# Gated attention and a Hyena convolution in one kernel: the last output stores move to GpSimd's queue, the spectrum's transfers are shared between two queues, the last tile is split, and the planner gets other weights

## The chip, the cores and the metric

The kernel runs on one core of a Trainium2 chip. The time is the device time of one launch in microseconds (us), lower is better. The engines are called as in the profile: PE (TensorE, matmuls; PEld is its weight load), DVE (VectorE), ACT (ScalarE), POOL (GpSimd) and SP (SyncE, which only issues transfers). Each engine executes its own list of instructions in order; an instruction that waits holds up all that stand behind it on the same engine. A transfer is issued by one of the engines and counts as one of that engine's instructions.

## The reference

Batch B = 8, sequence S = 3136, width D = 256, width of the queries 64. The inputs are u, v, z, and the weights `w_proj`, `filter_fft`, `w_out`.

```python
def _attn_ref(u, v, z):
    scale = 1.0 / S
    scores = scale * np.matmul(z, z.transpose(0, 2, 1))
    attn = np.maximum(scores, 0.0) ** 2
    out = np.matmul(attn, v)
    return u * out

def _moe_ref(x, w_proj, filter_fft, w_out):
    proj = x @ w_proj
    x1, x2, x3 = proj[..., :D], proj[..., D:2*D], proj[..., 2*D:]
    X2 = np.fft.rfft(x2, n=S, axis=1)
    H = np.fft.rfft(filter_fft, n=S, axis=0)[None, :, :]
    x2_conv = np.fft.irfft(X2 * H, n=S, axis=1)
    y = x1 * x2_conv * x3
    return y @ w_out
```

The first function's result is the x of the second. The output has the shape (8, 3136, 256) in float32.

## The kernel before

**The work of a batch.** The 3136 columns of the score matrix are cut into seven chunks (512 five times, 256, 320). For each chunk, tiles of 128 rows of scores are computed by matmuls that use 64 rows of the array (z has 64 columns), two or four of them side by side in the halves or quarters of the array, into one of three pairs of PSUM banks (`ps_s`). ACT takes the relu into `R_t` (L1767), DVE (L1776) or ACT (L1774) squares it into `A_t`, and PE weighs v with it: matmuls of the full array into `ps_o_t`. All matmuls go through one helper and carry its line, L521. Some tiles are not computed but transposed from their mirror image (`M_t`, `M1_t`, `M2o_t`, `M2e_t`). When a chunk is through, DVE multiplies by u (`xT_t`, L1818), and three projections follow: two of them become a gate (a copy `x_t` by ACT, L554, and a product `gate_t` by DVE, L1160), and the third goes into the spectrum.

**The convolution.** It is a DFT of 3136 = 64 x 49 points as matrix products. The first step of each chunk yields `s_t`, which SP writes to a buffer D1 in DRAM (L964; the profile calls it `spec`). With all chunks of a batch written, `add_spectrum` loads it back in another order (`load_spec`, L994), does eight forward quads (matmuls of half the array), copies (L554 on ACT, L558 on DVE) into `xh`, multiplies with the filter's spectrum H on DVE (L1248), does the inverse quads, and writes the result to a second DRAM buffer, D2 (`put`, L1293; three transfers for each set of quads, cut by rows in `by_row`). `add_end` loads that (`load_c`, L1006), does the last DFT step (called conv below), multiplies with the gates on DVE (`yT_t`, L1334), multiplies with w_out, copies the result out of PSUM in tiles of two (L554, L558) and stores it (`store`, L1394: two transfers a chunk, one for each half of the rows).

**What sets the order.** The order of every engine's instructions is made when the program is built, by a planner in Python (classes `Task` and `Plan`). A task has a cost in microseconds for each engine that may do it (two engines for copies and squares), tasks that it depends on, buffers that it takes, `moves` (the time that its transfer occupies the modelled transfer engines) and `late` (an addition to the modelled arrival). `Plan.go` always starts the task that can begin first in the model, and so writes the lists. These estimates only decide the order and which of two engines does a copy or a square; on the chip semaphores guard the data. `pick_pe` chooses PE's next task among scores (S), quads (Q), weigh matmuls (W) and the convolution's and the output's matmuls (FA, FB, FZ), by the numbers of a `Rule`:

- `backlog`: how much weigh work must be waiting before other work is taken while scores wait for a PSUM pair
- `ample`: from how much waiting weigh work on scores are done in groups of three and not two
- `stay`: how long PE may wait for further scores before it leaves the half-array mode
- `first`: how much weigh work must be waiting for a quad to be put ahead of scores
- `lead`: how many scores must have run before a quad may follow in the same stretch
- `pace`: how much credit for other work each weigh task earns
- `full`: from which load of ACT and DVE on other work stands behind the weigh work
- `give`: in `pick`, the penalty on a second engine's taking over a task, for the time that it holds up tasks which only it can do

**The end of the program.** The last chunks of the last batch but one (from chunk `HOLD` = 3 on) are held back in the queue FZ, where they fill PE's gaps in the last batch; their outputs come from cut pieces of `v_t` (the class `Cut`) and from `ost_t`. The last batch (`final`) puts its spectrum in five sets, two quads, two, two, one and one, from the buffers `gs_t`, `gs_t`, `M2o_t`, `A_t` and `uT_t`. Its chunks end in the order `FINAL` = 0, 2, 4, 6, 1, 3, 5; there, with `split`, POOL stores the first half of the rows and SP the second, except for the last chunk, which SP stores in one piece for each pair of tiles. In the steady part SP issues all output stores, spectrum transfers and transposing loads, and POOL the loads of u (`un_t`, L595) and v (`v_t`, L614).

Of the kernel before, what the change touches and what calls it, by code (L numbers as in the profile page):

```python
# [27 lines left out]
LATE_PUT, LATE_LOAD, LATE_TURN, LATE_C, LATE_D2 = 3.0, 1.0, 1.5, 2.5, 1.0  # L28
SPEC_LAG = 1
LATE_F = 6.0  # L30
LATE_OUT = 2.0
AFTER = (1, 3, 5, 6)
FINAL = (0, 2, 4, 6, 1, 3, 5)
ZP, ZL = 0, 0.0
# [1 line left out]
REACH = 2  # L36
Rule = namedtuple("Rule", "backlog ample stay first lead pace full give")
STEP = 50.0
RULES = [Rule(0.5, 5.0, 0.15, 0, 1, 0.55, 3.5, 0)]
SHARE = {0: 1, 2: 3}  # L40

ISSUED = "issued"
# [349 lines left out]
def kernel(  # L392
# [10 lines left out]
    nc = tc.nc  # L403

    B, S, D = u.shape
# [9 lines left out]
    home = {t: c for c in range(NC) for t in tiles[c]}  # L415
# [8 lines left out]
    D2 = [dram.tile([NT * P, D], BF16, name=f"spec2_{i}") for i in range(2)]  # L424
# [123 lines left out]
    def on(engine, emit, cost, deps=(), takes=(), **kw):  # L548
        return job(None, lambda e: emit(), {engine: cost}, deps, takes, **kw)
# [168 lines left out]
    for i, (t0, t1) in enumerate(zip(z_cuts, z_cuts[1:])):  # L718
        step_ = -(-(t1 - t0) // -(-(t1 - t0) // 8))
        for g0 in range(t0, t1, step_):  # L720
            nt = min(step_, t1 - g0)
            box = {}
# [260 lines left out]
    def by_row(d, t, x0, n):  # L983
        rows = d[0:S, :].rearrange("(q r x) d -> r q x d", r=2, x=2 * NJ)[:, :, ds(x0, n), :]
        got = [(rows[r, 0:EVEN], t[ds(r * N1, EVEN), 0:n, :]) for r in range(2)]
        return got + [(rows[:, EVEN], t[EVEN : EVEN + N1 + 1 : N1, 0:n, :])]

    def load_spec(src, j0, nj, deps, late=0.0, home=l_p):
        box = {}

        def go():
            box["t"] = home.tile([P, 8, D], BF16)
            for rows, part in by_row(src, box["t"], 2 * j0, 2 * nj):
                nc.sync.dma_start(out=part, in_=rows)  # L994

        t = on("SP", go, 1.3, [*deps, *((d, ISSUED) for d in loads[-1:])], [home.slots], moves=0.6 * nj, late=late)
        return in_order(t), box

    def load_c(src, c, deps, home):
        t0, nt = T0[c], len(tiles[c])  # L1000
        box = {}

        def go():
            box["t"] = home.tile([P, 4, D], BF16)
            view = src[ds(t0 * P, nt * P), :].rearrange("(t p) d -> p t d", t=nt)
            nc.sync.dma_start(out=box["t"][:, 0:nt, :], in_=view)  # L1006

        if home is c_p:
            return in_order(on("SP", go, 0.45, [*deps, *((d, ISSUED) for d in loads[-1:])], [home.slots], moves=0.4 * nt, late=LATE_C)), box
        return on("SP", go, 0.45, deps, [home.slots], moves=0.4 * nt), box  # L1010

    def sides(x):
        return x[:, 0:D], x[:, D : 2 * D]
# [200 lines left out]
    def add_spectrum(b, puts):  # L1214
        deps0 = list(h_done) + list(tz_done) if b == 0 else []
        final = b == B - 1
        sets = [(0, 1), (2, 3), (4, 5), (6,), (7,)] if final else [(0, 1), (2, 3), (4, 5), (6, 7)]
        set_of = {g: x for x in sets for g in x}
        outs = [gs_p, gs_p, M_p[2], A_p, uT_p] if final else [gs_p] * 4
        homes = [l_p, l_p, *M_p[:2]]  # L1220
        lasts = []
        behind = []
        ldb, gb = [None], [None]
        for g in range(NJ // 2):
            own = not final or g % 2 == 0
            xh = xh_p if own else R_p
            mine = set_of[g]
            per, gh = 2 * len(mine), outs[sets.index(mine)]
            if g % 2 == 0:
                ldb[0] = load_spec(D1[b % 2], 2 * g, 4, puts, LATE_LOAD * (not final), homes[g // 2] if final else l_p)  # L1230
            ld, ibox = ldb[0]
            xb = {}

            def mm(ps, g=g, xb=xb, ibox=ibox, xh=xh):
                xb["x"] = xh.tile([P, 2, 4, D], BF16)
                forward(ps, slot(ibox["t"], 2 * g % 4), g)

            def ev(e, h, p, xb=xb):
                copy(e, xb["x"][:, 0, ds(2 * h, 2), :].rearrange("p c d -> p (c d)"), p)

            a0, evs = add_quads(mm, ev, c_quads(g), [ld, *deps0], [xh.slots])
            if g % 2:
                a0.frees.append((ld, 0))

            def mul(i, g=g, xb=xb):
                x = xb["x"][:].rearrange("p i (j c) d -> p i j c d", c=2)
                h = H[:, ds(2 * g, 2), i].unsqueeze(2).to_broadcast([P, 2, 2, D])
                nc.vector.tensor_tensor(x[:, 1 - i], x[:, 0], h, ALU.mult)  # L1248

            def add(xb=xb):  # L1250
                x = xb["x"][:].rearrange("p i (j c) d -> p i c j d", c=2)
                nc.vector.tensor_tensor(x[:, 1, 0], x[:, 1, 0], x[:, 0, 1], ALU.subtract)
                nc.vector.tensor_tensor(x[:, 1, 1], x[:, 1, 1], x[:, 0, 0], ALU.add)

            cost = c_dve2(4 * D)
            w_ = on("DVE", lambda mul=mul: mul(0), cost, evs, prio=ZP)
            w_ = on("DVE", lambda mul=mul: mul(1), cost, [w_], prio=ZP, lat=ZL)
            z_ = w_ if final else on("DVE", add, 2 * c_dve2(2 * D), [w_], prio=ZP)

            def inv(g=g, xb=xb, z_=z_, a0=a0, gh=gh, mine=mine, per=per):  # L1260
                new = g == mine[0]
                if new:
                    gb[0] = {"es": [], "firsts": []}
                gx = gb[0]

                def mm(ps, g=g, new=new):
                    if new:
                        gx["g"] = gh.tile([P, 2 * per, D], BF16)
                    z, y = (slot(xb["x"][:, i], 0) for i in range(2))
                    if final:  # L1270
                        inverse2(ps, y, z, g)
                    else:
                        inverse(ps, y, g)

                def ev(e, h, p, g=g):
                    copy(e, gx["g"][:, ds(2 * (2 * (g - mine[0]) + h), 2), :].rearrange("p c d -> p (c d)"), p)

                a, evs = add_quads(
                    mm, ev, c_quads(g, 1 + final), [z_, *gx["firsts"], *(minus_task if final else [])], [gh.slots] if new else []
                )  # L1280
                gx["firsts"] = [a]
                if new:
                    gx["g0"] = a
                a.frees.append((a0, 1))
                inverses.append(a)
                gx["es"] += evs
                if g != mine[-1]:
                    return
                j0 = 2 * mine[0]

                def put():
                    for rows, part in by_row(D2[b % 2], gx["g"], 2 * j0, 2 * per):
                        nc.sync.dma_start(out=rows, in_=part)  # L1293

                p_ = on("SP", put, 1.2, gx["es"], moves=0.5 * per, late=LATE_D2 * (not final))
                p_.frees.append((gx["g0"], 1))
                lasts.append(p_)

            behind.append(inv)
            if g >= SPEC_LAG:  # L1300
                behind.pop(0)()
        for x in behind:
            x()
        return lasts

    def add_end(b, lasts, gtasks, cs, kind="FB", src=c_p, dsts=(o_p,), late=0, behind=(), then=(), split=False, mids=(y_p,)):
        for at, c in enumerate(cs):
            t0, nt = T0[c], len(tiles[c])
            w = CHUNKS[c]
            dst, mid = dsts[at % len(dsts)], mids[at % len(mids)]  # L1310
            ld, cb = load_c(D2[b % 2], c, lasts, src)
            yb = {}
            ys = []
            firsts = []
# [33 lines left out]
                ys.append(e_)  # L1348
            ob = {}
            oe = []  # L1350
            for i0 in range(0, nt, 2):
                n = min(2, nt - i0)
                last = min(P, w - (i0 + n - 1) * P)
                box = {}

# [34 lines left out]
            def store(i0, n, only=(0, 1), by=nc.sync, c=c, ob=ob):  # L1390
                r = rows_n1(out[b])
                for j, lo, hi, n2 in runs(T0[c] + i0, T0[c] + i0 + n):
                    if j in only:
                        by.dma_start(out=r[:, n2 : n2 + hi - lo, :], in_=ob["o"][ds(j * N1, N1), i0 : i0 + hi - lo, :])  # L1394

            if split and c == cs[-1]:
                for k, e_ in enumerate(oe):
                    s_ = on("SP", lambda i0=2 * k, n=min(2, nt - 2 * k), store=store: store(i0, n), 0.9, [e_, *behind], prio=1, moves=0.9)
            elif split:
                s_ = on("POOL", lambda nt=nt, store=store: store(0, nt, (0,), nc.gpsimd), 0.6, [*oe, *behind], moves=0.22 * nt)  # L1400
                s_ = on("SP", lambda nt=nt, store=store: store(0, nt, (1,)), 0.8, [*oe, *behind], prio=1, moves=0.22 * nt)
            else:
                s_ = on("SP", lambda nt=nt, store=store: store(0, nt), 1.3, [*oe, *behind], prio=1, moves=0.45 * nt, late=LATE_OUT * (dst is o_p))
# [508 lines left out]
```

## Time and profile before

| what | value |
|---|---|
| median of 3 runs | 992.51 us (992.26 to 992.87) |
| the profiled execution's own time | 993.72 us |
| its span | 991.5 us |
| mean granted clock of PE | 0.99 |
| packets under 512 B | 242442 of 332343 |
| mean transfer rate | 172 GB/s |
| relus on ACT, L1767 | 512, busy 466.9 us, mean 963 ns |
| squares on DVE, L1776 | 283 of the main form's group, 313.9 us, mean 1123 ns |
| squares on ACT, L1774 | 213 of the main form's group, 211.7 us, mean 1007 ns |
| copies `x_t` on ACT, L554 | 148, 81.7 us, mean 583 ns |
| multiplications with H on DVE, L1248 | 120, 82.0 us, mean 683 ns |

The page of the profile shows one execution, so its span is set against that execution's own time and not against the median. "Busy" is the time in which an engine executes; the sum over engines exceeds the span as they run side by side. The chain that ended last is put down to PE for 82% of the span, to DVE for 7% and to ACT for 4%. A row such as the relu's also names what the engine had waited for: ACT sat idle 57.1 us before relus, 55.0 of them for PE's scores.

### The profile page before, as it was taken

The page shows a single profiled execution, that of the slowest core. Times are in us where ns is not written, and L with a number is a line of the kernel's source. Part 1 is how long each engine was busy: PE and PEld are TensorE (multiplying, and loading weights), DVE is VectorE, ACT ScalarE, POOL GpSimd, SP SyncE. Part 2 cuts the span into 40 slices and gives each one's busy share as a digit, 9 for nine tenths or more (in the row PEclk, how much of TensorE's full clock was granted, in tenths as well). Part 3 has the DMA queues.
Part 4 walks back from the last instruction along what each step waited for, and adds up shares of the span by engine and source line. Part 5 has one row for each costly group of instructions (what it writes and reads, how often), then busy time and mean ns, then how long its engine had stood idle before and what let it go on. Part 6 is the DMA issues. An engine that isn't in the chain of part 4 may idle for free.

```text
span 991.5 us, 19534 instructions
## 1 busy us (share of the span) xinstructions
PE 958.2 (97%) x6831; PEld 472.2 (48%) x6831; DVE 819.4 (83%) x1465; ACT 867.9 (88%) x1187; POOL 191.7 (19%) x409
## 2 busy tenths in 40 slices
PE   6999999999999999999999999999999999999985
PEld 2344544455444554446444454444544455544643
DVE  7876689987899878987789877898779988799774
ACT  6988898988998898899989999889989899999773
POOL 5132311132013210313111220121202231001001
PEclk9999999999999999999999999999999999999978
DMA  9889958979979799978998786998889978984576
GB/s 154 150 171 199 165 118 128 187 137 185 202 174 176 147 194 187 186 156 133 200 197 178 148 152 152 205 191 158 153 196 186 203 138 165 202 213 106 154 229 197
DMA packets 332343, 170.32 MB, mean 172 GB/s; under 512 B 242442, under 2 KB 307786, under 8 KB 332244
## 3 DMA queue, kind: packets, MB, share of 16 engines
q1 hardware_dynamic: 304068, 136.59, 63.4%
q0 software_dynamic: 28176, 32.48, 23.2%
q8 instruction: 54, 0.88, 0.4%
q14 instruction: 45, 0.37, 0.1%
HBM read 90.26 MB, written 53.35 MB: 145 GB/s over the span
## 4 chain that ended last, share of the span: by engine, by line
PE 82%; DVE 7%; ACT 4%; DMA 2%; issue 2%; SPq 1%; POOL 0%; POOLq 0%; DVEq 0%; ACTq 0%
PE ps_o_t L521 48%; PE ps_s L521 34%; DVE A_t L1776 2%; ACT R_t L1767 2%; DVE xT_t L1818 1%; DMA M2e_t<-A_t 1%; DVE xh L1248 1%; DMA ost_t<-in_z_dram 1%; DMA conv_in_t<-spec 1%; DVE gate_t L1160 1%; DVE yT_t L1334 1%; SPq L646 1%; ACT A_t L1774 0%; ACT x_t L554 0%; DMA M_t<-A_t 0%
## 5 line engine op out<-in xcount | busy, mean ns | idle before, releaser
L1767 ACT ACTIVATE R_t<-ps_s 128x1024 f32<-128x1024 f32 (+4 forms) x512 | 466.9, 963 | 57.1 <-PE ps_s L521 55.0
L521 PE MATMUL ps_o_t<-A_t,v_t 128*128 128x512 bf16 (+3 forms) x2084 | 459.5, 354 | 2.9 <-DVE A_t L1776 2.1
L521 PEld LDWEIGHTS <-v_t 128*128 128x128 bf16 (+2 forms) x2878 | 250.6, 98 | 257.8 <-issue 73.2
L1776 DVE TENSOR_TENSOR A_t<-R_t 128x1024 bf16<-128x1024 f32 (+3 forms) x283 | 313.9, 1123 | 64.2 <-ACT R_t L1767 61.1
L1774 ACT ACTIVATE A_t<-R_t 128x1024 bf16<-128x1024 f32 (+3 forms) x213 | 211.7, 1007 | 3.1 <-DMA M2e_t<-A_t 1.7
L521 PE MATMUL ps_s<-zT_t 64*64 64x512 bf16 (+5 forms) x1485 | 170.8, 361 | 2.0 <-ACT R_t L1767 1.0
L604 POOL COPY tick<-xT_t 1x1 bf16<-1x1 bf16 x54 | 13.8, 256 | 681.6 <-DVE xT_t L1818 681.6
L521 PEld LDWEIGHTS <-zT_t 64*64 64x64 bf16 (+1 forms) x1518 | 53.9, 101 | 109.7 <-issue 93.7
L521 PE MATMUL ps_s<-xT_t,wp 128*128 128x512 bf16 (+2 forms) x430 | 103.7, 353 | 2.4 <-DVE gate_t L1160 0.9
L554 ACT ACTIVATE x_t<-ps_s 128x512 bf16<-128x512 f32 (+2 forms) x148 | 81.7, 583 | 19.7 <-PE ps_s L521 12.5
L1818 DVE SCALAR_TENSOR_TENSOR xT_t<-ps_o_t,uT_t 128x256 bf16<-128x256 f32 (+2 forms) x224 | 76.1, 381 | 22.8 <-PE ps_o_t L521 14.4
L1248 DVE TENSOR_TENSOR xh<-xh,H 128x1024 bf16<-128x1024 bf16 x120 | 82.0, 683 | 2.1 <-ACT xh L554 0.9
L521 PE MATMUL ps_o_t<-M_t,v_t 128*128 128x512 bf16 (+2 forms) x352 | 81.8, 353 | 0.0
L1160 DVE TENSOR_TENSOR gate_t<-ps_s,x_t 128x256 bf16<-128x256 f32 (+2 forms) x216 | 71.2, 381 | 6.6 <-PE ps_s L521 4.6
L1334 DVE TENSOR_TENSOR yT_t<-ps_s,gate_t 128x512 bf16<-128x512 f32 (+2 forms) x99 | 57.9, 613 | 10.3 <-PE ps_s L521 10.0
L558 DVE CAST xh<-ps_s 128x512 bf16<-128x512 f32 x71 | 47.3, 685 | 22.8 <-PE ps_s L521 19.5
L521 PEld LDWEIGHTS <-wp 128*128 128x128 bf16 x448 | 42.3, 98 | 49.6 <-issue 15.2
L595 POOL DMA_DIRECT2D un_t<-in_u_dram x112 | 59.8, 554 | 5.6 <-issue 2.7
L614 POOL DMA_DIRECT2D v_t<-in_v_dram x112 | 59.4, 552 | 6.4 <-issue 3.8
L521 PE MATMUL ps_s<-wp,xT_t 128*128 128x256 bf16 x398 | 56.7, 272 | 0.5 <-ACT R_t L1767 0.3
L521 PE MATMUL ps_s<-wo,yT_t 128*128 128x256 bf16 (+1 forms) x344 | 52.0, 273 | 1.6 <-DVE yT_t L1334 1.3
L554 ACT ACTIVATE s_t<-ps_s 128x512 bf16<-128x512 f32 (+1 forms) x79 | 44.9, 592 | 5.5 <-PE ps_s L521 2.1
(154 smaller groups left out, 833.1 us busy)
## 6 DMA issues: line engine op xcount, KB each, us to landing
out_dram<-ost_t SPq DMA_DIRECT2D x66, 256.0 KB
spec<-s_t SPq DMA_DIRECT2D x96, 128.0 KB
spec_in_t<-spec SPq DMA_DIRECT2D x60, 192.0 KB
spec<-gs_t SPq DMA_DIRECT2D x60, 192.0 KB
v_t<-in_v_dram POOLq DMA_DIRECT2D x80, 128.0 KB, 4.5
un_t<-in_u_dram POOLq DMA_DIRECT2D x80, 128.0 KB, 4.9
conv_in_t<-spec SPq DMA_DIRECT2D x33, 256.0 KB
out_dram<-ost_t SPq DMA_DIRECT2D x19, 128.0 KB
```

The lines of the kernel that those rows point to most:

```text
L521: wrote(nc.tensor.matmul(o, *args, **kw), o)
L554: got = nc.scalar.activation(out_, in_, AF.Copy)
L558: got = nc.vector.tensor_copy(out_, in_)
L595: nc.gpsimd.dma_start(out=t[ds(j * N1, N1), lo - t0 : hi - t0, :], in_=x[:, n2 : n2 + hi - lo, :])
L614: nc.gpsimd.dma_start(out=t[ds(j * N1, N1), ds(v_at(a), (b - a) * D)], in_=r[:, n2 + a - lo : n2 + b - lo, :].rearrange("p t d -> p (t d)"),)
L1160: got = nc.vector.tensor_tensor(g[:, ::-1] if h == 0 else g, p, x, ALU.mult)
L1248: nc.vector.tensor_tensor(x[:, 1 - i], x[:, 0], h, ALU.mult)
L1334: got = nc.vector.tensor_tensor(yb["y"][:, dh, 0:w], p, gates[b, c, dh][:, 0:w], ALU.mult)
L1767: has_read(nc.scalar.activation(blocks(box["R"], n, cw)[:rows], p, AF.Relu), p)
L1774: nc.scalar.activation(a, r, AF.Square)
L1776: nc.vector.tensor_tensor(a, r, r, ALU.mult)
L1818: nc.vector.scalar_tensor_tensor(x, f, inv_s2, ut, ALU.mult, ALU.mult)
```

## The change

Five things are edited; the rest of the code is the same.

1. The `Rule` has other numbers (`backlog` 0.5 to 1.25, `stay` 0.15 to 0.05, `first` 0 to 0.5, `pace` 0.55 to 0.5, `full` 3.5 to 3.0, `give` 0 to 1.0).
2. The planner's estimates of two loads are others: `load_spec` (issue 1.3 to 1.6, transfer 0.6 to 0.4 for each) and `load_c` outside its own pool (0.45 to 0.55, 0.4 to 0.3).
3. In the last batch each set's put to D2 is divided: SP issues the first one or two of its three transfers, POOL the rest. Over the five sets that makes eight by SP and seven by POOL.
4. All output stores of the last batch but one are issued by POOL, 14 of them after the last of POOL's loads.
5. The last chunk of the last batch (chunk 5, two tiles) computes, copies out and waits for its output tile by tile (`step` = 1); one half of its rows is stored by SP, the other by ACT.

```diff
+LATE_POOL = 1.2
...
-RULES = [Rule(0.5, 5.0, 0.15, 0, 1, 0.55, 3.5, 0)]
+RULES = [Rule(1.25, 5.0, 0.05, 0.5, 1, 0.5, 3.0, 1.0)]
...
-        t = on("SP", go, 1.3, [*deps, *((d, ISSUED) for d in loads[-1:])], [home.slots], moves=0.6 * nj, late=late)
+        t = on("SP", go, 1.6, [*deps, *((d, ISSUED) for d in loads[-1:])], [home.slots], moves=0.4 * nj, late=late)
...
-        return on("SP", go, 0.45, deps, [home.slots], moves=0.4 * nt), box
+        return on("SP", go, 0.55, deps, [home.slots], moves=0.3 * nt), box
...
-                def put():
-                    for rows, part in by_row(D2[b % 2], gx["g"], 2 * j0, 2 * per):
-                        nc.sync.dma_start(out=rows, in_=part)
-
-                p_ = on("SP", put, 1.2, gx["es"], moves=0.5 * per, late=LATE_D2 * (not final))
+                def put(part=slice(0, 3), by=nc.sync):
+                    for rows, t in by_row(D2[b % 2], gx["g"], 2 * j0, 2 * per)[part]:
+                        by.dma_start(out=rows, in_=t)
+
+                if final:
+                    n = 1 + mine[0] // 2 % 2
+                    p_ = on("SP", lambda: put(slice(0, n)), 0.55 * n, gx["es"], moves=0.25 * per)
+                    lasts.append(
+                        on("POOL", lambda: put(slice(n, 3), nc.gpsimd), 0.55 * (3 - n), gx["es"], moves=0.25 * per, late=LATE_POOL)
+                    )
+                else:
+                    p_ = on("SP", put, 1.2, gx["es"], moves=0.5 * per, late=LATE_D2)
...
+            step = 1 if split and c == cs[-1] else 2
...
-            for i0 in range(0, nt, 2):
-                n = min(2, nt - i0)
+            for i0 in range(0, nt, step):
+                n = min(step, nt - i0)
...
             if split and c == cs[-1]:
-                for k, e_ in enumerate(oe):
-                    s_ = on("SP", lambda i0=2 * k, n=min(2, nt - 2 * k), store=store: store(i0, n), 0.9, [e_, *behind], prio=1, moves=0.9)
+
+                def both_queues(nt=nt, store=store):
+                    store(0, nt, (0,))
+                    store(0, nt, (1,), nc.scalar)
+
+                s_ = on("SP", both_queues, 0.6, [*oe, *behind], prio=1, moves=0.45 * nt)
+            elif b == B - 2:
+                s_ = on(
+                    "POOL", lambda nt=nt, store=store: store(0, nt, by=nc.gpsimd), 1.2, [*oe, *behind],
+                    moves=0.45 * nt, late=LATE_POOL,
+                )
```

The planner's cost of a task and its `moves` enter the order of all engines, so the edits change the order outside the places that they name, too.

## Prediction

> **What bounds the kernel now.** I read the page's totals and its 40 slices first.
>
> ```profile
> span 991.5 us, 19534 instructions
> ...
> PE 958.2 (97%) x6831; PEld 472.2 (48%) x6831; DVE 819.4 (83%) x1465; ACT 867.9 (88%) x1187; POOL 191.7 (19%) x409
> ...
> PE   6999999999999999999999999999999999999985
> ...
> PEclk9999999999999999999999999999999999999978
> ```
>
> PE is busy throughout except in the first slice and the last two, and only there is the clock lower. So the span is PE's time plus a start (11.6 us idle in the first 50, which the change leaves alone: PE's order there is the same) plus a tail. I then cut the rest into stages, one row each: from:to, length, then PE, PEld, DVE, ACT and POOL busy (instructions), granted clock, DMA share, GB/s.
>
> ```profile
> 50.00:900.00 850.00, 845.28 (x5948) 411.05 (x5947) 714.13 (x1250) 767.72 (x1035) 171.03 (x359) 1.00 0.90 173
> 900.00:931.40 31.40, 31.40 (x263) 17.73 (x261) 24.35 (x46) 27.79 (x41) 1.53 (x4) 1.00 0.53 130
> 931.40:946.90 15.50, 13.79 (x123) 9.53 (x120) 11.76 (x25) 9.67 (x18) 0.00 (x0) 1.00 0.65 170
> 946.90:963.50 16.60, 13.40 (x173) 8.04 (x173) 14.85 (x24) 13.24 (x27) 0.00 (x0) 0.63 0.82 247
> 963.50:971.80 8.30, 6.61 (x34) 3.27 (x33) 4.82 (x17) 3.99 (x8) 0.00 (x0) 0.91 0.53 151
> 971.80:982.50 10.70, 9.33 (x96) 7.14 (x95) 7.85 (x15) 6.91 (x13) 2.86 (x6) 1.00 0.82 244
> ```
>
> Steady part: PE idle 4.7 us of 850, so only a shorter instruction stream or a vanished wait pays. Then five stages of the last batch: last weighing; from its end (931.4) to the first forward quads; quads (DVE busy 14.85 of 16.6); gates; convolution and output. The queue of SP in the tail (start, length over all issues, instruction):
>
> ```profile
> 936.59 4.04 SPq L1394 DMA_DIRECT2D out_dram<-ost_t  x4
> 940.72 3.52 SPq L994 DMA_DIRECT2D spec_in_t<-spec  x6
> ...
> 964.54 1.32 SPq L1293 DMA_DIRECT2D spec<-uT_t  x3
> 967.09 4.09 SPq L1006 DMA_DIRECT2D A_t<-spec  x7
> ```
>
> Four output stores stand ahead of the spectrum's loads, and the loads of the convolution follow the last spectrum put.
>
> **A. More changes of mode, +1.8.** In the instruction lists as built, PE changes between half-array work (scores, quads) and full-array work 596 times instead of 578. What one change costs:
>
> ```profile
> 458.14 0.38 PE L521 MATMUL ps_o_t<-A_t,v_t 128*128 128x256 bf16 x2
> 458.46 0.45 PE L521 MATMUL ps_s<-zT_t 64*128 64x320 bf16 x4
> 458.83 1.70 PE L521 MATMUL ps_o_t<-A_t,v_t 128*128 128x256 bf16 x14
> ```
>
> Two matmuls of 256 stream in 2 x 0.109, yet the next group starts 0.32 later: +0.10. Four of 320, two side by side, take 2 x 0.136, the next starts 0.37 later: +0.10. 18 x 0.10 = +1.8 (1.5 to 2.2). Twelve extra matmuls are scores cut into quarters that run side by side: 0.
>
> **B. Waits in the steady part, -3.0.** The new weights move 20 of 218 squares from ACT to DVE and some 24 copies back. Squares: 1.08 us of 1024 on ACT, 1.22 on DVE; copies of 512: 0.61 and 0.685. ACT: -21.6 + 15 = about -7 us; DVE: +24.4 - 16.4 = +8. Of DVE's 64.2 us of idle before squares, 61.1 end with ACT's relu, and PE's starved moments end with ACT relus (1.9 us), DVE squares (2.1) and DVE gates (1.6). ACT is the fuller engine (767.7 against 714.1 of 850), so taking work off it should bring relus sooner. Counted from start to start, 22 gaps of PE over 0.2 us between 50 and 931 make 8.0 us: the lower bound is -8.0. The other bound: if DVE is what decides in the slices where its digit is 9 (11 of 40), 8 x 11/40 = +2.2. No row tells where the new order's gaps lie; I take the middle, -2.9, rounded to -3.0.
>
> **C and D. Work moved ahead of 931.4: +3.5, and -3.7 behind it.** After the last weigh matmul 387 matmuls are left instead of 423: 4 of gates at 0.216, 16 of conv at 0.055, 16 of output at 0.109 go ahead, 3.5 us of PE. There PE is 31.40 of 31.40 busy, so all of it counts (0 to 3.5). In the stage behind, 13.79 of 15.5 us are PE's, and DVE loses four yT of 512 and two gates of 256. The row that stands for the stage (its bracket is the idle time before it and its releaser):
>
> ```profile
> 942.59 0.69 DVE L1334 TENSOR_TENSOR yT_t<-ps_s,gate_t 128x512 bf16<-128x512 f32 x1 [0.91 <-PE ps_s L521]
> ```
>
> DVE's chained operations start 0.60 apart at 512 and 0.33 at 256: 4 x 0.60 + 2 x 0.33 = 3.1, and some 0.6 of such a wait goes with them: -3.7, to 11.8 us. This holds only if the data are there: spectrum puts leave SP at 935.9, landing 1.2 later as the uT put did (965.86 to 966.95), the first loads need 2.1 us of issue with no store between, land by at most 4.4: 943.9, or 12.6 us after 931.4, so -2.9 at the worst. If SP still had the four stores ahead, the loads would begin at 940.7 and nearly nothing would be gained. Bounds -4.5 and 0.
>
> **E. Quads, -1.2.** DVE is the bound there, and copies on it go from 8 to 6, two more on ACT (13.24 of 16.6 busy): 2 x 0.60 = -1.2 (-1.6 to 0). The eight output stores that SP issues from 947.74 to 956.2 go to POOL, which is empty there (0.00 busy). SP's first put starts at 956.31, directly after them, so they cover nothing that DVE's chain does not cover too.
>
> **F. Half clock, 0.** From 951.3 to 965.2 the granted clock is about 0.5. Earlier quads may move the drop: 1.7 us either way, a tenth of the quads' stage.
> A rule bears on it: the Trainium skill, "TensorE: Matmul & The Clock Gate", on the clock gate, has PE fall to half rate after a window of idling. Here PE was busy 2.5 of the 4.1 us before 951 and still fell; by that rule a stage without PE's idle moments would keep the full clock, and the sum would be up to 1.7 lower, 988.2.
>
> **G. The last tile, 0.** It is stored by SP and ACT, in single tiles, which may save up to 0.9 (a store's issue). But the end is elsewhere (count, minimum/median/maximum ns, first and last start):
>
> ```profile
> L1907 POOLq DRAIN  x3: 51/93/8449, 982.3 to 991.3; - x3
> L1907 SPq DRAIN  x3: 7/7/12, 988.1 to 991.0; - x3
> ```
>
> POOL's drain starts at 982.31, lasts 8.449 to 990.76; SP is through at 988.05. 2.7 us of cover, so 0 (-0.9 to 0).
>
> **H. Spectrum puts by POOL, 0.** Seven of 15 puts go there, behind 14 stores on that queue. POOL's transfers land 3.7 to 5.3 us after issue (its stores at the end), SP's put in about 1.2: 2.5 to 4.1 late for the last one. SP's own last put becomes shorter (2 issues for 3, 0.44). The loads of the convolution could wait; the first began at 967.09 and its matmuls at 970.72, when gates still kept PE busy. Cover: some 1.2 us after the shorter SP issue; if that is gone, +2 (0 to +2). What waits behind the loads on SP is the output stores of the last batch only, first needed after 975.
>
> **Sum.** +1.8 - 3.0 + 3.5 - 3.7 - 1.2 = -2.6 on the profiled 993.72 (span 991.5 and 2.2 around it). The median is 1.2 below the profiled one; I take the difference onto it: 992.51 - 2.6 = **989.9**.
>
> **Rivals.**
> 1. *DVE becomes the bound* (slower). Place: squares and gates in the steady part. For it: DVE has up to 46.5 busy of 50 us (150 to 200) and gets 8 more; against it: ACT is fuller on the mean. It decides if PE's waits for DVE's squares grow past those for relus that vanish. 992.5 + 1.8 + 2.2 + 3.5 - 3.7 - 1.2 = 995.1.
> 2. *The gain is given back*: waits shrink by little (B at -0.5), and quads start when the spectrum lands (D at -2.9): 992.5 + 1.8 - 0.5 + 3.5 - 2.9 - 1.2 = 993.2. For it: C and D are the same work moved, worth only PE's 1.7 us of idle.
> 3. *Most gaps vanish*, B at -6: 986.9. For it: the weights are what sets PE's order everywhere; against it: 18 more changes of mode say that PE leaves its scores sooner, not that it waits less.
> 4. *POOL's puts starve* (slower). In the quads' stage DVE multiplies almost back to back (0.68 each, 948.6 to 961.3). If POOL's transfers only get going after it, half of the 14 stores and all seven puts are left: 14 x 0.55 us of issue (POOL's rows: 0.526 to 0.55) from 961.3 is 969.0, +4.4 to land, 973.4 against 966.95: 6.4 late, 1.2 covered: 989.9 + 5.2 = 995.1. No POOL transfer ran in that stage, so no row decides; against it, POOL's loads in the steady part landed within 5.3 with DVE 83% busy.
> The rule behind this is the Trainium skill's "SBUF — State Buffer", in the box on the "DVE blocks DMA" trap: GpSimd can't write descriptors while DVE holds their shared port in its fast modes. It speaks against giving spectrum puts to POOL.
>
> **How the numbers follow.** Forecast 0.42 (own range 987 to 990.4); most gaps vanish 0.10; given back 0.18 (991 to 994); DVE bound 0.24; POOL's puts 0.06. About 0.2%, 2.0 us, can be told from no change: under 990.5 is faster, 0.52; within 0.18; over 994.5 0.30. The range takes the gaps at their best with the half clock (986.9 - 1.4 = 985.5) and the DVE bound with 0.9 more for F or H (996.0).
>
> **What would show it.** Right: puts of s_t followed at once by spectrum loads on SP; 931.4's stage at 11 to 12.6 us; under 3 us of PE idle in 50:900; convolution's loads not later relative to the gates; the end still POOL's drain. Wrong: waits of PE for DVE squares longer than before; DVE's digits at 9 in more slices; the stage before the last weigh matmul longer by 3.5 with no shorter one behind; landings of POOL's spectrum puts over 6 us; the half clock over a longer stretch.

## The result and the profile after

The changed kernel takes 997.0 us (median of 14 runs, 994.3 to 1001.4), the kernel before 992.5 (14 runs, 991.6 to 995.4): a ratio of 1.0047 with a 95% interval of 1.0033 to 1.0061. It became slower by about half a percent. The prediction said 989.9 and a range up to 996.0.

The profiled execution of the changed kernel was the fastest of the 14, 994.34 us with a span of 992.6. Read alone it hides most of the loss, so a second profiled execution of the same program was taken (span 996.4, first experiment). The page of the first, in the same lines as before:

```profile
span 992.6 us, 19518 instructions
...
PE 945.9 (95%) x6746; PEld 471.2 (47%) x6843; DVE 830.4 (84%) x1462; ACT 861.2 (87%) x1191; POOL 205.7 (21%) x430
...
PE   6998999999999999999999999999999999999974
...
PEclk9999999999999999999999999999999999999978
```

PE has 6746 matmul records for 6843 weight loads: 97 records are missing, so PE's busy time and its small idle gaps "by issue" can't be set against those of before. I therefore read positions: when the last weigh matmul ends, when the first quad starts, and so on. DVE is 11 us busier and ACT 6.7 us less; the built lists had said +8 and -7.

The stages, cut at the same events (columns as in the prediction):

```profile
935.90:947.00 11.10, 10.00 (x91) 6.89 (x90) 8.45 (x19) 6.93 (x14) 3.48 (x7) 1.00 0.61 176
947.00:964.00 17.00, 12.30 (x171) 7.58 (x172) 13.68 (x22) 14.21 (x29) 5.03 (x10) 0.74 0.69 222
```

and of the second execution:

```profile
937.90:949.00 11.10, 10.03 (x89) 6.88 (x86) 8.46 (x19) 6.86 (x14) 3.40 (x7) 1.00 0.62 181
949.00:968.10 19.10, 12.24 (x173) 6.96 (x172) 13.68 (x22) 14.09 (x29) 5.06 (x10) 0.75 0.62 192
```

The stage behind the last weigh matmul shrank from 15.5 to 11.1 us in both. In the quads' stage DVE lost 1.2 us of work (14.85 to 13.68), and yet the stage did not become shorter: 17.0 and 19.1 us against 16.6. The queue of SP and that of POOL, first execution, show what else happened there:

```profile
941.00 3.10 SPq L995 DMA_DIRECT2D spec_in_t<-spec  x6
944.15 1.93 SPq L995 DMA_DIRECT2D M_t<-spec  x3
946.12 3.73 SPq L995 DMA_DIRECT2D M2e_t<-spec  x3
```

```profile
941.25 1.06 POOL L1403 DMA_DIRECT2D out_dram<-ost_t  x2 [6.09 <-ACT ost_t L555]
943.71 1.05 POOL L1403 DMA_DIRECT2D out_dram<-v_t  x2 [1.40 <-ACT v_t L555]
945.63 2.10 POOL L1403 DMA_DIRECT2D out_dram<-v_t  x4 [0.87 <-ACT v_t L555]
947.90 1.05 POOL L1403 DMA_DIRECT2D out_dram<-ost_t  x2 [0.18 <-issue]
```

The puts of `s_t` are now followed at once by the loads, as forecast. But POOL's stores run beside these loads, not behind them. In the kernel before, the loads of `M_t` and `M2e_t` took SP 1.42 and 1.58 us to issue, here 1.93 and 3.73. The second execution, SP and then a wait of PE:

```profile
946.17 3.86 SPq L995 DMA_DIRECT2D M_t<-spec  x3
950.07 3.12 SPq L995 DMA_DIRECT2D M2e_t<-spec  x3
```

```profile
PE ps_s L522 <- DMA M_t<-spec: 4.1, 1, 4.1
```

PE waits 4.1 us for the load into `M_t`; in the first execution 2.0, in the kernel before not at all. How full the transfers are shows in a cut of two microseconds, first the kernel before and then the changed one (last columns: granted clock, DMA share, GB/s):

```profile
947.00:949.00 2.00, 1.66 (x21) 0.77 (x21) 1.61 (x3) 1.92 (x5) 0.00 (x0) 1.00 0.99 260
```

```profile
947.00:949.00 2.00, 1.81 (x20) 0.71 (x19) 1.42 (x3) 1.97 (x5) 1.78 (x4) 1.00 1.00 381
```

The transfer engines are full in both. In the changed kernel stores share them with loads that PE is about to need; in the kernel before the last of these loads leaves SP at 947.35, and PE needs it only at 954.3. And the end of the program (L1925 is the same place as L1907 before):

```profile
L1925 POOLq DRAIN  x3: 51/93/10084, 981.6 to 992.2; - x3
L1925 SPq DRAIN  x3: 7/13/120, 988.3 to 992.2; - x3
```

POOL's drain (an instruction at the end of its list) still ends last, but it takes 10.08 us instead of 8.45.

### The profile page after: what moved, and what is told of

It reads as the page before. It is cut to its first block, busy times and chain, and to the rows that moved or that the text cites. A ratio compares the mean times of both kernels' runs of the same rounds, so it can differ in the third digit from the quotient of the medians.

```text
span 992.6 us, 19518 instructions
## 1 busy us (share of the span) xinstructions
PE 945.9 (95%) x6746; PEld 471.2 (47%) x6843; DVE 830.4 (84%) x1462; ACT 861.2 (87%) x1191; POOL 205.7 (21%) x430
## 4 chain that ended last, share of the span: by engine, by line
PE 78%; DVE 9%; issue 5%; DMA 3%; ACT 2%; SPq 1%; POOL 0%; POOLq 0%; DVEq 0%; ACTq 0%
PE ps_o_t L522 45%; PE ps_s L522 33%; DVE A_t L1794 3%; ACT R_t L1785 1%; DVE xT_t L1836 1%; DMA M2e_t<-A_t 1%; DVE xh L1249 1%; DMA M_t<-A_t 1%; DMA ost_t<-in_z_dram 1%; DVE gate_t L1161 1%; DVE xh L559 1%; DMA M_t<-spec 1%; SPq L647 1%; DVE gs_t L559 0%; DVE yT_t L1343 0%
## 5 line engine op out<-in xcount | busy, mean ns | idle before, releaser
L522 PE MATMUL ps_o_t<-A_t,v_t 128*128 128x512 bf16 (+4 forms) x1993 | 447.7, 354 | 9.2 <-issue 4.3
L1794 DVE TENSOR_TENSOR A_t<-R_t 128x1024 bf16<-128x1024 f32 (+3 forms) x306 | 343.2, 1133 | 63.0 <-ACT R_t L1785 62.3
L522 PEld LDWEIGHTS <-v_t 128*128 128x128 bf16 (+1 forms) x2878 | 251.3, 98 | 259.7 <-issue 69.0
L1792 ACT ACTIVATE A_t<-R_t 128x1024 bf16<-128x1024 f32 (+3 forms) x190 | 186.0, 990 | 5.9 <-issue 2.4
L522 PE MATMUL ps_s<-zT_t 64*64 64x512 bf16 (+4 forms) x1497 | 174.2, 367 | 2.6 <-ACT s_t L555 1.3
L605 POOL COPY tick<-xT_t 1x1 bf16<-1x1 bf16 x54 | 16.9, 313 | 697.6 <-DVE xT_t L1836 697.6
L555 ACT ACTIVATE x_t<-ps_s 128x512 bf16<-128x512 f32 (+2 forms) x156 | 86.0, 585 | 25.6 <-PE ps_s L522 18.5
L555 ACT ACTIVATE s_t<-ps_s 128x512 bf16<-128x512 f32 (+1 forms) x92 | 53.7, 602 | 6.3 <-PE ps_s L522 4.6
L522 PE MATMUL ps_s<-wo,yT_t 128*128 128x256 bf16 (+1 forms) x366 | 54.9, 273 | 0.9 <-DVE yT_t L1343 0.8
```

The costliest lines, as they stand in the source:

```text
L522: wrote(nc.tensor.matmul(o, *args, **kw), o)
L555: got = nc.scalar.activation(out_, in_, AF.Copy)
L1792: nc.scalar.activation(a, r, AF.Square)
L1794: nc.vector.tensor_tensor(a, r, r, ALU.mult)
```

## The experiments

The changed edits fall into three groups: the planner's weights (W), its load estimates (L), and the end edits (E: stores and puts by POOL, the split last tile). Ratios are against the kernel before, run on the same chip, with 95% intervals. "Waits" is the end of the last weigh matmul less the time that the built list of PE needs up to there (each matmul at its streaming time, each change of mode at about 0.1 us). The count of changes also holds those between scores and weigh matmuls of 64 rows, which cost next to nothing (see A below). So these waits are too small by 8 to 9 us in both orders, and by 1.4 us more with the changed kernel's order than with that of before.

**The changed kernel again.** No edit.

> The changed kernel unaltered, for a second profiled execution: the first one took 994.3 us, the fastest of 14 runs (median 997.0, up to 1001.4), so it does not show the usual loss. Theory S (the loss lies in the steady part, in PE's waits under the new order): the median is again 996 to 998, and a profiled execution near it shows the last weigh matmul at 938 to 941 instead of 936.2, with 4 us or more of PE idle in the steady part added. Theory T (the loss lies in the tail, in transfers that POOL issues): the last weigh matmul ends at 936 again and the tail behind it is 3 us or more longer than 56.

997.2 us (6 runs), ratio 1.0053 (1.0036 to 1.0069); span 996.4. The last weigh matmul ended at 937.9 instead of 935.9, the tail behind it took 58.5 us instead of 56.7: both theories have a part. The tail's part is PE's wait for the spectrum; the other part is a stretch of half clock in the steady part (see B below).

**The weights alone.**

```diff
-RULES = [Rule(0.5, 5.0, 0.15, 0, 1, 0.55, 3.5, 0)]
+RULES = [Rule(1.25, 5.0, 0.05, 0.5, 1, 0.5, 3.0, 1.0)]
```

> The kernel before with the new weights alone: 582 changes of mode (578 before, 596 after), 22 squares fewer on ACT, 40 matmuls fewer behind the last weigh matmul. Theory S with the weights as the cause: 995 to 998 and a spread of several us between runs, PE waits in the first batch as in the changed kernel (1.5 and 1.3 us at 82 and 97 us). Theory T: 991 to 993, spread as before. My prediction's sum: +0.4 for the modes, -3 for waits, +3.9 for matmuls ahead, and nothing gained behind since SP still has stores ahead of the loads: 993.8.

992.1 us, ratio 0.9999 (0.9987 to 1.0011). The last weigh matmul ended 6.3 us later than before and the tail was 6.0 shorter (54.1). So the weights by themselves are a wash, and my working for them is wrong in two places that cancel: the waits did not shrink, and the tail gained more than I gave it although the stores still stood ahead of the loads (SP's first load came 5.1 us behind the last weigh matmul, as in the changed kernel, since SP could issue the stores while it waited for `s_t`).

**The old weights in the changed kernel** (L and E).

> The changed kernel with the old weights (load estimates, POOL's stores and puts and the split last tile stay): 564 changes of mode, squares 227 on ACT and 285 on DVE. Theory S with the weights as the cause: 989 to 992. Theory S with the load estimates as the cause: 995 to 998. Theory T: 995 to 998 with the tail longer than before.

997.9 us, ratio 1.0054 (1.0040 to 1.0068). The loss does not need the new weights.

**The end edits alone.**

> The kernel before with the edits at its end alone (stores and puts by POOL, the last tile split; old weights, old load estimates): PE's order up to the last weigh matmul is that of before. Theory T: 995 to 998. Theory S: 990.5 to 992.5, as SP's loads start earlier by up to 4 us but DVE's products of the convolution decide in the stage behind the last weigh matmul.

993.3 us, ratio 1.0007 (0.9999 to 1.0016): between the two theories. Here too SP issued the loads of `M_t` and `M2e_t` slowly (2.20 and 2.33 us), but the first of the spectrum's loads stood 6.3 us behind the last weigh matmul and the first quad 15.5, so nobody waited. POOL's drain took 9.77 us.

**The load estimates alone.**

```diff
-        t = on("SP", go, 1.3, ..., moves=0.6 * nj, late=late)
+        t = on("SP", go, 1.6, ..., moves=0.4 * nj, late=late)
-        return on("SP", go, 0.45, deps, [home.slots], moves=0.4 * nt), box
+        return on("SP", go, 0.55, deps, [home.slots], moves=0.3 * nt), box
```

> The kernel before with the new load estimates alone (564 changes of mode, squares 227 on ACT and 285 on DVE). Theory L (with the old weights the estimates give an order in which PE waits in the steady part: in the run with old weights the last weigh matmul ended 9.9 us later than before): 996 to 999, last weigh matmul at 940 to 942. Theory E (the end edits cost it whenever less work is left behind the last weigh matmul, since their stores run beside the spectrum's loads): 992 to 994.

996.2 us, ratio 1.0036 (1.0022 to 1.0051), as theory L said, the last weigh matmul at 939.6. With the old weights the estimates cost 7 us of waits (19.6 against 12 to 13), of which the tail gives 5.7 back.

**Weights and estimates, no end edits.**

> New weights and new load estimates without the end edits: PE's order is that of the changed kernel up to the last tile, but SP keeps all stores and puts. Theory E: 992 to 994, with the spectrum's loads issued at the usual pace (1.4 to 1.6 us for three) and no wait of PE for a load over 1.5 us. Theory L: 996 to 998, the last weigh matmul at 936 to 938 as in the changed kernel and the tail as long as there (56 to 58).

996.5 us, ratio 1.0040 (1.0027 to 1.0054). The time fits theory L, but its place does not: the waits up to the last weigh matmul were 12.0, by this count as in the kernel before. The planner put two more output stores ahead of the spectrum's loads on SP (the first load at 6.3 us behind the last weigh matmul, not 5.1), and PE waited for a load of `spec_in_t` 0.4 and 1.6 us. A third wait, 1.2 us ahead of the quads from `M_t`, is put down to a copy by ACT.

**Weights and end edits, old estimates.**

> New weights and the end edits with the old load estimates. Theory E: 995 to 997, as the weights leave the same 34 conv matmuls behind the last weigh matmul and POOL's stores run beside the spectrum's loads: a tail of 56 to 58 us, where the weights alone had 53.8. Theory L: 991 to 993.

996.0 us, ratio 1.0035 (1.0022 to 1.0048), as theory E said: a tail of 56.6 us, where the weights alone had 54.1. So the end edits, nearly free with the old weights, cost 3.9 us with the new ones, by the medians.

**The stores back on SP.** The branch for `b == B - 2` taken out of the changed kernel.

> The changed kernel with the 14 output stores of the last batch but one back on SP, eight of them behind the spectrum's loads; the spectrum's puts stay divided between SP and POOL, the last tile split; PE's order is the changed kernel's. Theory E with the stores as the cause: 992.5 to 994.5. Theory E with POOL's puts as the cause: 995 to 997. Theory L: 996 to 998.

997.6 us, ratio 1.0047 (1.0031 to 1.0063): no gain. Six stores then stood ahead of the loads on SP, and PE waited 0.3, 2.4 and 1.0 us for loads. Within these intervals the kernel is as slow with stores ahead of the loads as with stores beside them.

**The stores behind the loads.** In the changed kernel, POOL copies one element of the last spectrum load before it issues the eight stores of the held-back chunks:

```diff
+                        landed = on("POOL", lambda: await_x(last_box), 0.1, last_spec)
-                        add_end(b - 1, early, held[1], range(HOLD, NC), "FZ", cut_in, outs, 4, [(last_spec[0], ISSUED)], [q_])
+                        add_end(b - 1, early, held[1], range(HOLD, NC), "FZ", cut_in, outs, 4, [(last_spec[0], ISSUED), landed], [q_])
```

> The changed kernel with one more instruction on POOL: a copy of one element of the last spectrum load, ahead of the eight stores from the cut pieces and the last tile of the held-back batch, so that these start only when the spectrum has landed (on SP they stood behind its loads; PE's order is the changed kernel's). Theory stores: the stores that run beside the loads make them late; PE's waits for M_t's load (2.0 and 4.1 us in the two profiled executions) fall under 1.5 us, the quads' stage from 15.4 and 17.5 to 14 to 15 us, the median to 994 to 995.5. Theory chain: the loads are late because the last s_t put comes 4.1 us behind the last weigh matmul and the first quad 11.1 us behind it; waits and median (996 to 998) stay.

995.0 us, ratio 1.0019 (1.0006 to 1.0033), where the changed kernel had 1.0047 and 1.0053. PE's list is the changed kernel's. The timeline of POOL and then of SP:

```profile
952.88 0.58 POOL L605 COPY tick<-M2e_t 1x1 bf16<-1x1 bf16 x1 [9.14 <-DMA M2e_t<-spec]
953.40 2.10 POOL L1405 DMA_DIRECT2D out_dram<-v_t  x4
```

```profile
942.42 3.02 SPq L997 DMA_DIRECT2D spec_in_t<-spec  x6
945.49 1.54 SPq L997 DMA_DIRECT2D M_t<-spec  x3
947.07 2.44 SPq L997 DMA_DIRECT2D M2e_t<-spec  x3
```

SP's issue of the `M_t` load is near its pace in the kernel before (1.54 us for 1.42), that of `M2e_t` still slower (2.44 for 1.58). PE waited 0.6 us for `spec_in_t` and no longer for the `M_t` load: the 1.4 us ahead of those quads are put down to a copy by ACT. The last quad came 15.3 us after the first, a little more than the 14 to 15 expected. The theory of the stores holds for the larger part; the theory of the chain keeps some 2 us of wait that are there without the stores.

**POOL's stores of the last batch only for its first three chunks**, in the kernel before:

```diff
-            elif split:
+            elif split and at < 3:
                 s_ = on("POOL", ...
```

> The kernel before, but of the last batch's stores POOL issues only those of the first three chunks; SP issues both halves of the others. Theory drain: the end is set by POOL's drain, 8.4 us from POOL's last transfer; it then starts near 978.5 and is over before SP's last wait, the span ends 2 us earlier and the median is 990 to 991. Rival: the drain waits for all transfers, whoever issues them, and ends as late as before: 992 to 993.

991.3 us, ratio 0.9987 (0.9974 to 0.9999). In the kernel before the drain set the end; now SP does:

```profile
L1907 POOLq DRAIN  x3: 46/93/8556, 976.7 to 988.2; - x3
L1907 SPq DRAIN  x3: 7/7/13, 987.7 to 988.0; - x3
```

The drain starts at 976.7 and is over 8.6 us later, at 985.2, while SP waits until 987.7 for its own transfers. From PE's last matmul to the end it is 8.1 us instead of 9.7.

**The same with the new weights.**

> The same with the new weights. Theory drain: 2 us under the weights alone (992.1): 990 to 991. Rival: 992 to 993.

989.4 us, ratio 0.9969 (0.9959 to 0.9980): faster than both kernels. The last quad comes 14.3 us after the first, the end 8.0 us after PE's last matmul.

**The split last tile alone.**

> The kernel before with the split last tile alone (single tiles, half of the rows stored by SP and half by ACT; POOL's instructions are those of before). If the split tile lengthens POOL's drain: 9.6 to 10 us of drain as in all kernels with the end edits, 993 to 994. If POOL's additional transfers lengthen it: 8.4 us and 991.5 to 992.5.

993.2 us against 993.1, ratio 1.0002 (0.9992 to 1.0012); the drain 8.74 us. Neither gain nor loss; the drain comes near the second theory.

**Both repairs in the changed kernel**: the stores held behind the loads, and POOL's last stores ended early.

> The changed kernel with both repairs: the held-back batch's stores wait on POOL for the last spectrum load, and POOL issues the last batch's stores of the first three chunks only. Theory (stores beside the loads, and the end set by POOL's drain, are the two causes that the end edits add): 2 to 3 us under the run with the stores held alone (995.0): 992 to 993, level with before. Rival (something in the order of weights and estimates together costs as much): 994 to 996.

992.6 us against 992.1, ratio 1.0003 (0.9988 to 1.0017): level with before, as the theory said. This does not show that the two causes are the whole loss. Ending POOL's stores early is a gain without the end edits, too: with it the kernel before has 0.9987 and the weights alone 0.9969 (0.9959 to 0.9980). Against the latter, which has the same end of POOL's stores, the changed kernel with both repairs is still 0.34% slower, clear of both intervals.

**POOL's additions one by one**, in the kernel before: the 14 stores,

> The kernel before with the last batch but one's 14 output stores on POOL, nothing else. If these lengthen POOL's drain: 9.6 us or more instead of 8.4, 993 to 994. The first quad stays at 15.5 us behind the last weigh matmul, since DVE's products set it.

and the seven puts.

> The kernel before with the spectrum's puts of the last batch divided between SP and POOL, nothing else. If the seven puts lengthen POOL's drain: 9.6 us or more, 993 to 994. My prediction's term H, that the later landing of POOL's puts is covered by the gates: the time from the last quad to the first conv matmul stays at 8.7 us; if not, up to 2 us longer.

992.5 us, ratio 0.9998 (0.9989 to 1.0007), and 993.3 us, 1.0006 (0.9993 to 1.0019): neither can be told from before. The drain took 9.04 us with the stores and 8.86 with the puts, 8.74 with the split tile and 9.77 with all three, against 8.45. Each adds 0.3 to 0.6, none alone the 1.3; both expectations of one cause fail. What the two texts say of the tail came true: the first quad stayed 15.5 us behind the last weigh matmul with the stores, the first conv matmul 8.7 us behind the last quad with the puts. (Kernels without any of the three had drains up to 9.2, so the single steps are no more than a hint.) The stores alone show their effect on SP, with nobody waiting for it:

```profile
940.06 3.03 SPq L995 DMA_DIRECT2D M_t<-spec  x3
943.15 2.47 SPq L995 DMA_DIRECT2D M2e_t<-spec  x3
```

With the puts alone these six loads take 2.80 us (1.38 and 1.42), with the stores 5.50.

## Why the prediction was wrong, point by point

Where the time lies, in us; each row is read from the timelines, and each column adds up to its span but for rounding:

| stage | before | forecast | changed, first | changed, second | stores behind loads | both repairs | weights alone | weights, POOL early |
|---|---|---|---|---|---|---|---|---|
| to the last weigh matmul | 931.4 | +2.3 | 935.9 | 937.9 | 937.3 | 937.7 | 937.7 | 937.7 |
| to the first quad | 15.5 | -3.7 | 11.1 | 11.1 | 11.1 | 11.1 | 9.8 | 9.8 |
| to the last quad | 15.1 | -1.2 | 15.4 | 17.4 | 15.3 | 14.7 | 14.9 | 14.3 |
| to the first conv matmul of the last batch | 8.7 | 0 | 8.7 | 8.4 | 8.5 | 8.4 | 8.7 | 8.1 |
| to PE's last matmul | 11.1 | 0 | 10.2 | 10.2 | 10.2 | 10.2 | 11.1 | 11.1 |
| to the end | 9.7 | 0 | 11.3 | 11.3 | 10.8 | 8.8 | 9.7 | 8.0 |

In the order of their size the misses are these. Up to the last weigh matmul the changed order of PE takes 6.3 us more, on the mean of six profiled executions of each order, where the forecast had 2.3 (A and B). The quads take 0.2 and 2.3 us more, where it had 1.2 less (E). The end takes 1.6 us more, where it had nothing (G).

**A, right in its price and wrong in its count; C, right.** A change between 128-row and 64-row matmuls does cost 0.09 to 0.10 us. But the count of 596 and 578 takes weigh matmuls of 64 rows, which stand between scores, for full-array work. The kernel before shows one such place:

```profile
925.84 0.31 PE L521 MATMUL ps_s<-zT_t 64*128 64x320 bf16 x2
925.99 0.30 PE L521 MATMUL ps_o_t<-A_t,v_t 64*128 64x320 bf16 x2
```

The starts are 0.15 us apart, and two such matmuls side by side stream in 0.136. Counted by the rows of the array, in the executions that have all records, PE changes 498 times in the kernel before and 502 times in the changed one (494 and 500 up to the last weigh matmul). So A is worth +0.4 to +0.6, not +1.8. The matmuls ahead of the last weigh matmul came to 3.9 us by the built lists; I had 3.5.

**B failed, and it is the largest miss.** The step was to take PE's waits for shorter under the new order, by 3.0 us. Six executions with the changed kernel's order of PE waited 11.0 to 13.4 us up to the last weigh matmul (mean 12.3), six with the order of before 11.6 to 13.0 (mean 12.15), the start included: +0.15 by the count above, and about +1.5 when only the changes that cost something are counted. The new order has waits in the first batch, near 83 and 98 us, that the old one does not have there: 1.48 and 1.33 us in the first execution of the changed kernel, 0.25 and 2.39 in the second. One of each, and a stretch of the second (columns as for the stages):

```profile
84.08 0.38 PE L522 MATMUL ps_s<-xh,T 128*128 128x512 bf16 x1 [1.48 <-ACT R_t L1785]
```

```profile
98.36 0.88 PE L522 MATMUL ps_s<-zT_t 64*128 64x256 bf16 x6 [2.39 <-ACT s_t L555]
```

```profile
98.50:101.90 3.40, 3.40 (x13) 1.23 (x10) 2.14 (x2) 3.03 (x5) 0.00 (x0) 0.50 0.81 83
```

In the second execution PE was busy for 2.11 of the 4.5 us up to 98.5, and then ran at half clock for 3.4 us, in the steady part. In the first it was busy for 3.20 of them, and the clock stayed at 1.00. Such a stretch of half clock, between 84 and 104 us, stands in six of the nine profiled executions with the new weights and in none of the six with the order of before. Among the six with the changed kernel's order, the three that have it end their last weigh matmul at 937.3 to 937.9, the three without it at 935.6 to 936.5: 1.7 us apart on the mean, half of 3.4. That is most of the 2.0 us between the two executions of the changed kernel up to there. The prediction looked for the half clock in the tail alone (F).

PE's waits for `xT_t`, which the page of before hardly shows, grew as well (before, then the changed kernel):

```profile
PE ps_o_t L521 <- DVE xT_t L1818: 0.5, 1, 0.5
PE ps_s L521 <- DVE xT_t L1818: 0.4, 2, 0.2
```

```profile
PE ps_o_t L522 <- DVE xT_t L1836: 2.1, 6, 0.5
PE ps_s L522 <- DVE xT_t L1836: 1.5, 7, 0.3
```

They went from 0.9 to 3.6 us. DVE's additional squares may cause them; that was not tried by itself. Taking the middle between -8.0 and +2.2 made a term of three microseconds out of not knowing.

**D, right.** -4.4 for -3.7; the first quad did follow the loads. My bound from the landing (12.6 us) was about the first set of loads. I did not follow the third set, and it is there that PE waits. The bound itself is added up wrongly: 935.9 + 1.2 + 2.1 + 4.4 is 943.6, not 943.9.

**E failed.** The step was the sentence that the eight output stores "cover nothing" where SP issued them. (In the rows they are ten, 2 + 6 + 2; eight are those of the held-back chunks.) They did something there: SP's order held them behind the spectrum's loads. In the code this guard is `behind`, a dependency on the loads being issued, which orders the planner's model and, on SP, the queue. On POOL's queue nothing on the chip waits for SP's issue, so the stores start when their tiles are ready, those of the held-back chunks from 943.7 on, and share full transfer engines with the loads. I had DVE as the bound of the quads, and its work did fall by 1.2 us; the bound had become the load of the third set: 2.0 and 4.1 us of wait. Holding the stores back returned about 3 us by the medians. Giving them back to SP returned nothing; two more of them than with the weights alone then stood ahead of the loads, and PE waited for loads again.

**F and H, right.** In the tail the clock was at half for 10.2 us in both executions of the changed kernel, in two stretches, and for 13.6 in the kernel before. The gates' stage kept its length. POOL's puts landed in 2.1 to 3.7 us in both executions of the changed kernel, and in at most 5.6 in the other kernels that have them. In the kernels where POOL issues them the last quad stands 8.4 to 9.0 us ahead of the first conv matmul; it is 8.7 in the kernel before and 7.6 to 8.7 in all where SP issues them. So rival 4 did not happen. One of its arguments was misread: POOL's loads in the steady part landed in up to 9.3 us, not within 5.3. The rule named beside it (the Trainium skill, "SBUF — State Buffer", the box on the "DVE blocks DMA" trap) finds nothing here (it speaks of DVE's fast modes, and no row shows whether these multiplies run in one): the changed kernel's puts landed sooner than the 3.7 to 5.3 us of POOL's stores at the end of before, with DVE 13.7 us busy of 17.0.

**G failed in sign.** I had 2.7 us of cover under POOL's drain, and took its length as given. It grew by 1.6 us in both executions of the changed kernel, and as it is what ends the program, that counted in full. The conv stage gave 0.9 back that I had not foreseen (11.1 to 10.2); kernels with the old estimates have it at 11.1, so it comes with the estimates' order and not with the split tile (11.1 alone).

**The rivals.** The one that gave nearly the measured time, DVE as the bound of the steady part (995.1), is not what happened: the longest new waits of PE in the steady part end with ACT. Its place, more waits in the steady part, was nearer than B's. "Given back" had the right place, the spectrum's chain behind the last weigh matmul, but not what made the chain longer. The forecast's tail of -4.9 came out as -3.4 and -1.6, the part before it as +4.5 and +6.5. (The range's lower end takes 1.4 us for the half clock, where F has 1.7; nothing else hangs on it.)

**What stays open.** No single group of edits carries the loss. Without the end edits the changed kernel has 1.0040, without the new estimates 1.0035, without the new weights 1.0054, and the estimates alone have 1.0036. So with the new weights the end edits cost some 4 us where the estimates are old, and about 1 us where these are new, too. Weights and estimates without the end edits lie 4.4 us above the weights alone by their medians, and only 1.4 by their profiled spans (993.2 and 991.8). Of these two executions only the one with the weights alone has the early half clock, and the mean clock of the executions behind the medians differs (0.987 and 0.992); no profile shows where they lost it. The changed kernel's executions have 0.989 and 0.990 to 0.991 in the median, those of the kernel before 0.992 to 0.993, so a part of the loss may lie in the clock; that was not tried. Nor did I find why the load estimates cost 7 us of waits with the old weights and none with the new.

## What to carry to other kernels

When a transfer moves to another queue, look for what the old queue's order held back: an order that was free on one queue needs a wait on two. Where a profile shows an engine as a stage's bound, follow every load that the stage uses, not the first alone, before crediting a saving on that engine. And where a queue's drain ends the program, look first at when that queue issues its last transfer: ending POOL's stores three chunks early gained 0.1 to 0.3% here, where all the edits of the change together lost 0.5%. Last, where two executions of one program differ, compare the granted clock stage by stage before looking for another cause.

## What the runs showed of the hardware that was not expected

SP's issue of a transfer went with what another queue did: the last six spectrum loads took SP 2.8 to 4.0 us to issue with POOL quiet, and 4.5 to 7.0 where POOL's stores were issued ahead of them and beside them. In the one run where POOL's stores began in the middle of these loads (the old weights in the changed kernel) they took 3.0. In the two microseconds shown above, 0.99 and 1.00 of the transfer engines were busy, at 260 and 381 GB/s. POOL's drain at the end is no constant: 8.4 to 9.2 us in the six kernels without any added POOL transfer or split tile, 9.6 to 10.1 with all end edits; what it waits for, no run shows. A pause of PE in the steady part was followed by a slower clock: after 2.11 of 4.5 us busy came 3.4 us at 0.50. And one profiled execution can be the best of 14: the first one of the changed kernel lay 2.7 us under its median.
